# A decayed linear attention and two gated MLPs in one kernel: the last two attention chunks as 64x64 quarters of TensorE

## The chip, the cores and the metric

The kernel runs on one core of a Trainium2 chip. Its engines work side by side, each through its own list of instructions: TensorE (PE; PEld is its weight load), VectorE (DVE), ScalarE (ACT), GpSimd (POOL) and SyncE (SP), which issues the DMAs. The metric is the device time of one execution in microseconds; lower is better.

## The reference

`x` is the output of a block-wise linear attention with a decay for each head, and two MLPs follow on it. B = 2 batches, H = 8 heads, S = 768 tokens, D = 64.

```python
for b in range(nb):                      # blocks of 64 tokens
    intra = np.einsum('bhic,bhjc->bhij', qb, kb) * Dmask[None]     # lam ** (i - j), 0 above the diagonal
    intra = np.einsum('bhij,bhjd->bhid', intra, vb)
    inter = np.einsum('bhid,bhde->bhie', qb * lam_pow[None], kv_state)
    out[:, :, sl] = intra + inter
    kv_state = lam_block * kv_state + np.einsum('bhsd,bhse->bhde', kb * rev_pow, vb)
...
a = x @ w_a                              # 1536x512 by 512x1536
b = x @ w_b
x = (a * b @ w_out)
...
h = np.maximum(np.maximum(x @ w1, x @ w2), x @ w3)                 # 1536x512 by 512x768
return (h @ w_out)
```

## The kernel before

**Attention.** The kernel works on chunks of C = 128 tokens, NC = 6 of them for each batch. `n` numbers chunk and batch (n = 2m + b), and `pair(m)` is chunk m of both batches. For each n: `scores` multiplies keys with queries (PE), `masked` multiplies the result with the decay table (DVE, tiles `am`), `queries` and `keys` scale operands (POOL, in the tiles `aq` and `av`), `earlier` multiplies the running state `held` with the scaled queries (the state product, into the PSUM banks `o`), `within` adds the values, `taken` copies `o` into `x` (ACT), `update` multiplies scaled keys with values (into the bank `k`), and `carry` folds that into `held` (DVE; the tile is called `stt`). Heads are kept in halves of 64 partitions. From the fourth chunk on (`c >= SHORT`) `scores` leaves out the corner that the mask makes zero, and small bf16 matmuls on `warm` write zeros there, since `masked` still reads the whole square.

**First MLP.** Weights arrive as int64 words of 64-bit floats (`wr`), are converted to fp32 (`w` or `wd`, by three ACT passes and one DVE pass that joins them), combined by subtractions for a Strassen scheme, and split into a high and a low part (`hi` by an ACT copy, `lo` by a DVE or POOL subtraction); `x` is split in the same way (`x1A` are the parts of the second half of the tokens, `x0S` the parts of sums `x0s` of the first half). Every product is three matmuls: high by high, high by low, low by high. `plain_group` makes the first groups without Strassen; each `yield` of it is one layer block of 12 matmuls of 128x384 (L721, PSUM bank `p`), whose first half of columns ACT copies away (`z`) and whose second half DVE multiplies with it (`g`). The groups after that run seven products each (L701, banks `zu`, `bu`, `xu`).

**What sets the order.** The program is written out engine by engine. For PE, the loop over m at the end of the function writes the order down: scores, `next(layer1)` once or twice (one layer block each), `earlier`, `within`, `taken`, `update`, `carry`. `operands(1)` after the last chunk queues the splitting of x1. The work of ACT, DVE and POOL that isn't written out (weights, sums, splits) is placed between by `Pace`, a running estimate of each engine's time: a task's next step is issued when the estimate says that its engine is free. So other costs in the calls of `pace.pe` and `pace.run` move such steps to other places in the engines' lists, and sometimes from POOL to DVE (`EITHER`).

**PSUM.** There are eight banks, given out in turn. `results(m, apart)` takes two banks of `o` for a pair, or four when `apart`, which before holds for the last chunk alone.

Of the kernel before, what the change touches and what calls it, by code (L numbers as in the profile page):

```python
# [15 lines left out]
ALU = mybir.AluOpType  # L16
# [20 lines left out]
NPLAIN = 2  # L37
BYDVE = ()
SHORT = 3
NS = 26  # L40


# [126 lines left out]
def decay_attention_gated_mlps(ctx: ExitStack, tc: tile.TileContext, qkv: bass.AP, lam: bass.AP, wup: bass.AP, wdown: bass.AP, out: bass.AP):  # L169
# [9 lines left out]
    def slot(name, dt=F32):  # L179
        return sp.tile([128, 1536], dt, tag="s", name=name)  # L180
# [4 lines left out]
    def bank(name):  # L185
        return pp.tile([128, 512], F32, tag="ps", name=name)
# [7 lines left out]
    def copy(o, a):  # L194
        nc.scalar.activation(out=o, in_=a, func=AF.Copy)  # L195
# [267 lines left out]
    def pair(m):  # L463
        return 2 * m, 2 * m + 1
# [22 lines left out]
    def scores(n):  # L487

        q, k = aq[n][:, 0:512], aq[n][:, 512:1024]
        sc[n] = [bank(f"s{n}_{i}") for i in range(2)]  # L490
        if order[n][1] < SHORT:
            for a in range(NP):
                o = slice(128 * a, 128 * a + 128)
                for i in range(2):
                    nc.tensor.matmul(sc[n][i][:, o], k[rows(i), o], q[rows(i), o], start=True, stop=True)
            pace.pe(0.9, at["aq", n])
            return
        for a, late in ((0, 0), (0, 1), (1, 1), (1, 0), (2, 0), (2, 1), (3, 0), (3, 1)):
            for i in range(2):
                js = slice(128 * a + 64 * late, 128 * a + 64 * late + 64)  # L500
                o = slice(128 * a + 64 * late, 128 * a + 128)
                nc.tensor.matmul(sc[n][i][rows(late ^ a // 2), o], k[rows(i), js], q[rows(i), o], start=True, stop=True)  # L502
            if late and a % 2:
                p = a // 2
                for i in range(2):
                    o = sc[n][i][rows(1 - p), 256 * p:256 * p + 256].rearrange("p (a i) -> p a i", a=2)[:, :, 0:64]
                    nc.tensor.matmul(o, warm[rows(i), 0:64], warm[rows(i), 0:128], start=True, stop=True)
        pace.pe(0.8, at["aq", n])

    def masked(n):  # L510

        am[n] = slot(f"am{n}")
        for i in range(2):
# [20 lines left out]
        at["qs", n] = beside(512, at["aq", n])  # L534

    def keys(n):
        k, o = (av[n][:, x:x + 512].rearrange("p (h d) -> p h d", h=H) for x in (0, 1024))
        nc.gpsimd.tensor_tensor(out=o, in0=k, in1=decay[:, :, C - 1:C].to_broadcast([128, H, D]), op=ALU.mult)
        at["kd", n] = beside(512, at["av", n])
# [12 lines left out]

    def earlier(n):

        q = aq[n][:, 1024:1536]
        for w in range(2):
            for i in range(2):
                for x in range(2):
                    a = 2 * w + x
                    nc.tensor.matmul(  # L560
                        place(n, 4 * i + a), held[rows(i), n % 2, a], q[rows(i), 128 * a:128 * a + 128],
                        start=ob[n][1] == 0 and w == 0, stop=False, skip_group_check=True)
        pace.pe(0.5, max(at["qs", n], at["st"]))

    def within(n):

        v = av[n][:, 512:1024]
        for w in range(2):
# [9 lines left out]
    def update(n):  # L578

        if n % 2 == 0:  # L580
# [10 lines left out]
    def carry(m):  # L591

        src = kv[m].rearrange("p (b a e) -> p b a e", b=B, a=NP)
# [16 lines left out]
    def taken(n, *to):  # L610
        b, c = order[n]
        j = c // 3
        for x, name, dt in zip((xa, xh, xl), ("x", "xh", "xl"), (F32, F32R, F32R)):
            if (j, b) not in x and (j == 0 or x is xa):
                x[j, b] = slot(f"{name}{j}{b}", dt).rearrange("p (a i) -> p a i", a=KD)
        for x in to:
            for i in range(2):
                copy(tokens_of(x, n, i), result(n, i))
                at["x", n, i] = pace.run("ACT", 256, pace.t["PE"])
# [110 lines left out]
                    pace.run("DVE", J)  # L730
                yield

    def add(o, ps, z):
        nc.vector.tensor_tensor(out=o, in0=ps, in1=z, op=ALU.add)  # L734
        return pace.run("DVE", J)

    def tokens(j, b):
        return slice((2 * j + b) * J, (2 * j + b) * J + J)
# [210 lines left out]
    with tc.manual_schedule():  # L949
# [196 lines left out]
        for m in range(3, NC):  # L1146
# [27 lines left out]
            if m == 3:  # L1174
                pace.open(("x0", "sums"))
            if not last:
                for n in pair(m):
# [180 lines left out]
```

## Time and profile before

| | us |
|---|---|
| median of 3 runs | 502.0 (501.64 to 502.49) |
| span of the profiled execution, first to last instruction | 500.4 |
| PE busy | 493.1 |
| DVE busy | 345.8 |
| ACT busy | 293.9 |
| POOL busy | 58.1 |

For the profiled execution the trace gives the span; the device time of a run takes in what lies around it, and the median is 1.6 us above this span. Busy time is the union of an engine's instructions. A matmul's row starts when it begins to stream and lasts until its result is through, so successive matmuls overlap, and their rate is read from the distance of their starts.

### The profile page before, as it was taken

The page shows a single profiled execution, that of the slowest core. Times are in us where ns is not written, and L with a number is a line of the kernel's source. Part 1 is how long each engine was busy: PE and PEld are TensorE (multiplying, and loading weights), DVE is VectorE, ACT ScalarE, POOL GpSimd, SP SyncE. Part 2 cuts the span into 40 slices and gives each one's busy share as a digit, 9 for nine tenths or more (in the row PEclk, how much of TensorE's full clock was granted, in tenths as well). Part 3 has the DMA queues.
Part 4 walks back from the last instruction along what each step waited for, and adds up shares of the span by engine and source line. Part 5 has one row for each costly group of instructions (what it writes and reads, how often), then busy time and mean ns, then how long its engine had stood idle before and what let it go on. Part 6 is the DMA issues. An engine that isn't in the chain of part 4 may idle for free.

```text
span 500.4 us, 8186 instructions
## 1 busy us (share of the span) xinstructions
PE 493.1 (99%) x3348; PEld 465.0 (93%) x3348; DVE 345.8 (69%) x541; ACT 293.9 (59%) x458; POOL 58.1 (12%) x55
## 2 busy tenths in 40 slices
PE   8899999999999999999999999999999999999997
PEld 6799999999999999998888888999999999998897
DVE  6779869576576567567365079568877985787962
ACT  2677565564656553769572477545756456576461
POOL 3685301011111101110000000000000000000000
PEclk9999999999999999999999999999999999999999
DMA  8997002222221112314322021002202212110023
GB/s 285 407 410 270 3 0 85 84 85 84 86 84 59 35 56 64 126 54 151 134 84 86 0 84 56 29 1 84 67 20 84 86 63 64 63 65 0 22 106 126
DMA packets 10693, 46.93 MB, mean 94 GB/s; under 512 B 1312, under 2 KB 1568, under 8 KB 8096
## 3 DMA queue, kind: packets, MB, share of 16 engines
q1 hardware_dynamic: 10656, 46.41, 25.7%
q8 instruction: 26, 0.43, 0.4%
q14 instruction: 11, 0.09, 0.1%
HBM read 43.26 MB, written 3.15 MB: 93 GB/s over the span
## 4 chain that ended last, share of the span: by engine, by line
PE 95%; DMA 2%; DVE 1%; SPq 1%; issue 0%; ACT 0%
PE yp L820 20%; PE zu L701 18%; PE zv L701 15%; PE bu L701 9%; PE bv L701 7%; PE p L721 5%; PE out L874 5%; PE xu L701 4%; PE xv L701 4%; PE zo L923 3%; DMA av<-qkv_dram 2%; PE o L573 1%; PE bo L923 1%; PE s L502 1%; SPq L480 1%; PE xo L923 1%
## 5 line engine op out<-in xcount | busy, mean ns | idle before, releaser
L192 DVE TENSOR_TENSOR lo<-w,hi 128x1024 fp32r<-128x1024 f32 (+2 forms) x39 | 42.7, 1094 | 11.5 <-ACT hi L195 11.3
L195 ACT ACTIVATE hi<-w 128x1024 fp32r<-128x1024 f32 (+2 forms) x40 | 37.4, 935 | 14.2 <-DVE w L192 6.3
L820 PE MATMUL yp<-gh,dh 128*128 128x512 f32 x108 | 42.0, 389 | 0.0
L820 PE MATMUL yp<-gl,dh 128*128 128x512 f32 x108 | 42.0, 389 | 0.0
L820 PE MATMUL yp<-gh,dl 128*128 128x512 f32 x108 | 42.0, 389 | 0.0
L752 POOL TENSOR_TENSOR g<-z1u,z6u 128x384 f32<-128x384 f32 x21 | 22.6, 1076 | 148.2 <-DVE z6u L734 148.2
L192 DVE TENSOR_TENSOR gl<-g,gh 128x512 fp32r<-128x512 f32 x36 | 25.2, 720 | 20.7 <-ACT gh L195 20.7
L238 DVE SCALAR_TENSOR_TENSOR w<-ws,w 128x1024 int32<-128x1024 int32 (+1 forms) x21 | 30.7, 1464 | 9.6 <-ACT w L227 7.8
L227 ACT ACTIVATE w<-wr 128x1024 f16<-128x1024 f32 (+2 forms) x26 | 33.1, 1274 | 0.3
L192 DVE TENSOR_TENSOR w<-w 128x256 f32<-128x256 f32 (+1 forms) x57 | 30.1, 527 | 1.3
L222 ACT ACTIVATE w<-wr 128x1024 int32<-128x1024 uint16 (+2 forms) x26 | 27.5, 1056 | 2.4 <-DVE lo L192 2.0
L734 DVE TENSOR_TENSOR z6u<-bu,z6u 128x384 f32<-128x384 f32 x21 | 11.7, 556 | 21.0 <-PE bu L701 21.0
L195 ACT ACTIVATE gh<-g 128x512 fp32r<-128x512 f32 x36 | 21.4, 621 | 7.4 <-PE yp L820 7.4
L195 ACT ACTIVATE z6u<-zu 128x384 f32<-128x384 f32 x21 | 10.2, 484 | 24.9 <-PE zu L701 24.9
L820 PEld LDWEIGHTS yp<-gh,dh 128*128 128x128 f32 x108 | 20.3, 188 | 4.2
L820 PEld LDWEIGHTS yp<-gl,dh 128*128 128x128 f32 x108 | 20.3, 188 | 4.2
L230 ACT ACTIVATE ws<-wr 128x1024 f32<-128x1024 f32 (+1 forms) x22 | 24.1, 1094 | 0.2 <-DMA wr<-wup_dram 0.2
L820 PEld LDWEIGHTS yp<-gh,dl 128*128 128x128 f32 x108 | 20.3, 188 | 4.1
L195 ACT ACTIVATE z7u<-zu 128x384 f32<-128x384 f32 x21 | 10.3, 491 | 22.5 <-PE zu L701 22.5
L701 PE MATMUL bu<-x1S,hi 128*128 128x384 f32 x88 | 22.3, 334 | 0.0
L701 PE MATMUL zu<-x1S,hi 128*128 128x384 f32 x88 | 22.3, 334 | 0.0
L701 PE MATMUL zu<-x1A,hi 128*128 128x384 f32 x84 | 21.3, 334 | 0.0
(251 smaller groups left out, 1448.4 us busy)
## 6 DMA issues: line engine op xcount, KB each, us to landing
wr<-wup_dram SPq DMA_DIRECT2D x20, 1024.0 KB, 4.8
wr<-wdown_dram SPq DMA_DIRECT2D x12, 768.0 KB, 4.3
aq<-qkv_dram SPq DMA_DIRECT2D x12, 512.0 KB, 7.7
av<-qkv_dram SPq DMA_DIRECT2D x7, 512.0 KB, 11.0
out_dram<-ob SPq DMA_DIRECT2D x11, 256.0 KB, 2.0
av<-qkv_dram SPq DMA_DIRECT2D x7, 256.0 KB, 7.8
wr<-wup_dram SPq DMA_DIRECT2D x2, 512.0 KB, 9.7
out_dram<-ob SPq DMA_DIRECT2D x2, 128.0 KB, 1.9
```

Source lines behind the costliest of these rows:

```text
L192: (nc.vector if e == "DVE" else nc.gpsimd).tensor_tensor(out=o, in0=a, in1=b, op=op)
L195: nc.scalar.activation(out=o, in_=a, func=AF.Copy)
L222: nc.scalar.activation(out=w.bitcast(I32), in_=halves[:, :, 1], func=AF.Copy, scale=2.0 ** -13, bias=2.0 ** -14 - 0.5)
L227: nc.scalar.activation(out=o[:, :, 1], in_=high(double), func=AF.Copy, scale=2.0 ** -112)
L230: nc.scalar.activation(out=near, in_=high(double), func=AF.Copy, scale=2.0 ** -112)
L238: nc.vector.scalar_tensor_tensor(out=w, in0=near, scalar=3, in1=w, op0=ALU.logical_shift_left, op1=ALU.bitwise_or)
L701: nc.tensor.matmul(ps, w, x, start=p in FIRST and i == 0, stop=i == len(todo) - 1, skip_group_check=p not in FIRST)
L721: nc.tensor.matmul(ps, w[:, 128 * k:128 * k + 128], x[:, k], start=m == 0, stop=m == 11)
L752: nc.gpsimd.tensor_tensor(out=ga[g.n][:, tokens(g.j, 0)], in0=g.z[1], in1=g.z[6], op=ALU.mult)
L820: nc.tensor.matmul(ps[e], w[:, cols], g, start=k == 0 and m == 0, stop=k == K1 - 1 and m == 2)
L874: nc.tensor.matmul(ps, a[:, o:o + 128], w[:, s], start=k == 0 and n == 0, stop=k == K2 - 1 and n == 2)
L923: nc.tensor.matmul(ps, x[:, 128 * r:128 * r + 128], w, start=p in FIRST and n == 0, stop=n == 8, skip_group_check=p not in FIRST)
```

## The change

With `QUARTERS = 4`, the chunks c = 4 and 5 (n = 8 to 11) are computed on tiles of 64x64. On the host, keys and values of these chunks are laid out so that one half of the partitions holds both token halves of a head. Scores are written without the masked corner and without the zeros that filled it, 384 columns for four heads in place of 512; `near_table` copies the decay table in that form (four ACT copies after the fourth chunk's masks); `masked` multiplies 384 columns; `within` and `update` contract over 64 tokens at a time, in two halves of the partitions and two banks. Where the state product of a head and its values come from different partition halves, they land in different banks, and `taken` copies one (ACT) and adds the other (DVE). Both chunks take four banks for `o`. In the fifth chunk one of the two layer blocks moves from before the state product to between values and update.

```diff
@@ tables and masks
+    near = sttab[:, 640:1408].rearrange("p (h i) -> p h i", h=NP)
...
+    def near_table():
+
+        far = decay.rearrange("p (i r c) n -> p r i c n", i=2, r=2)
+        close = near.rearrange("p (i c) n -> p i c n", i=2)
+        for r in range(2):
+            s = slice(64 * r, 64 * r + 64)
+            for o, w in ((0, C), (C, 64)):
+                copy(close[s, :, :, o:o + w], far[s, r, :, :, 0:w])
+                pace.run("ACT", 4 * w)
...
@@ scores
+        if order[n][1] >= QUARTERS:
+            for c in range(2):
+                for late in range(2):
+                    for r in range(2):
+                        for p in range(2):
+                            a = 128 * (2 * r + c)
+                            nc.tensor.matmul(
+                                sc[n][p][rows(r), 192 * c + 128 * late:192 * c + 128 + 64 * late],
+                                k[rows(p), a + 64 * late:a + 64 * late + 64], q[rows(p), a + 64 * late:a + 128], start=True, stop=True)
+            pace.pe(0.65, at["aq", n])
+            return
@@ masked
+            for p in range(2):
+                nc.vector.tensor_tensor(out=am[n][:, 384 * p:384 * p + 384], in0=sc[n][p][:, 0:384], in1=near[:, 2 * p:2 * p + 2].rearrange("p h i -> p (h i)"), op=ALU.mult)
...
@@ earlier
+            for across in (1, 0):
+                for c in range(2):
+                    for p in range(2):
+                        r = p ^ across
+                        a, o = 2 * r + c, 256 if across else 128 * p
+                        nc.tensor.matmul(
+                            ob[n][0][p][rows(c), o:o + 128], held[rows(p), n % 2, a], aq[n][rows(p), 1024 + 128 * a:1152 + 128 * a],
+                            start=bool(across), stop=False, skip_group_check=True)
@@ within
+            for p in range(2):
+                for late in range(2):
+                    for c in range(2):
+                        for r in range(2):
+                            o, s = 256 * late + 128 * p + 64 * c, 384 * p + 192 * c + 128 * late
+                            nc.tensor.matmul(
+                                ob[n][0][r][rows(c), 128 * p + 64 * late:128 * p + 128], v[rows(r), o:o + 64], am[n][rows(r), s:s + 128 - 64 * late],
+                                start=False, stop=p == 1 and late == 1, skip_group_check=True)
+            pace.pe(0.7, max(at["av", n], at["am", n]))
+            return
@@ update
+                kv[n // 2] = [bank(f"k{n}_{i}") for i in range(2)]
...
+                            nc.tensor.matmul(
+                                kv[n // 2][r][rows(p), o:o + 64], k[rows(r), s:s + 64], v[rows(r), s:s + 64],
+                                start=n % 2 == 0 and c == 0 and late == 0, stop=n % 2 == 1 and c == 1 and late == 1, skip_group_check=True)
@@ taken
+        if c >= QUARTERS:
+            blocks = [xa[j, b][:, a, C * (c % 3):C * (c % 3) + C] for a in range(KD)]
+            banks = ob[n][0]
+            for r in range(2):
+                copy(blocks[2 - r], banks[1 - r][:, 256:384])
+                pace.run("ACT", 128, pace.t["PE"] - 0.7)
+            for r in range(2):
+                copy(blocks[3 * r], banks[r][:, 128 * r:128 * r + 128])
+                pace.run("ACT", 128, pace.t["PE"])
+                add(blocks[2 - r], banks[r][:, 128 - 128 * r:256 - 128 * r], blocks[2 - r], 128)
+            return
@@ the loop over the chunks
-            for _ in range(1 if last else 2):
+            if m == QUARTERS - 1:
+                near_table()
+            for _ in range(2 if m < QUARTERS else 1):
                 next(layer1)
-            results(m, last)
+            results(m, m >= QUARTERS)
...
             if not last:
+                if m >= QUARTERS:
+                    next(layer1)
                 for n in pair(m):
                     update(n)
                 carry(m)
```

The change moves instructions in the lists of DVE and ACT. The first place is DVE's list from the sixth chunk's masks (`am`) to the first low part of x1 (`x1A`), which the first layer block on x1 reads; `lo` is a weight's low part, `x0S` the low part of a sum of x0, `g` the product at a block's end. Before:

```order
L514 TENSOR_TENSOR am_868<-s_0_844,tables 128x512
L514 TENSOR_TENSOR am_868<-s_1_845,tables 128x512
L192 TENSOR_TENSOR wd_553<-wd_553 128x256
L192 TENSOR_TENSOR x0S_885<-x0s_431,x0S_885 128x768
L192 TENSOR_TENSOR wd_553<-wd_553 128x256
L192 TENSOR_TENSOR x1A_933<-x_610,x1A_933 128x768
```

And now:

```order
L538 TENSOR_TENSOR am_892<-s_1_875,stt 128x384
L193 TENSOR_TENSOR lo_910<-w_745,hi_909 128x1024
L193 TENSOR_TENSOR x0S_629<-x0s_431,x0S_629 128x768
L193 TENSOR_TENSOR lo_910<-w_745,hi_909 128x768
L822 TENSOR_TENSOR x_613<-o_0_914,x_613 128x128
L822 TENSOR_TENSOR x_613<-o_1_915,x_613 128x128
L822 TENSOR_TENSOR x_616<-o_0_916,x_616 128x128
L822 TENSOR_TENSOR x_616<-o_1_917,x_616 128x128
L193 TENSOR_TENSOR x0S_631<-x0s_431,x0S_631 128x768
L817 TENSOR_TENSOR g_705<-p_988,z_912 128x384
L193 TENSOR_TENSOR x1A_984<-x_613,x1A_984 128x768
```

The low parts of weight item 2 (`lo_910`; before, `lo_771` stood ahead of the masks on DVE and on POOL), two x0 sums and g now stand between the masks and x1A, beside the four new additions.

The second place is ACT's list in the same stretch, from weight item 2's high parts (`hi`) to x1's. Before:

```order
L195 ACTIVATE hi_770<-w_705 128x1024
L195 ACTIVATE x_610<-o_0_751 128x2x128
L195 ACTIVATE x_610<-o_1_752 128x2x128
L195 ACTIVATE x_613<-o_0_751 128x2x128
L195 ACTIVATE x_613<-o_1_752 128x2x128
L195 ACTIVATE hi_770<-w_705 128x768
L195 ACTIVATE z_886<-p_871 128x384
L195 ACTIVATE x0S_885<-x0s_431 128x768
L195 ACTIVATE x_610<-o_0_888 128x2x128
L195 ACTIVATE x_610<-o_1_889 128x2x128
```

And now:

```order
L196 ACTIVATE z_912<-p_895 128x384
L196 ACTIVATE hi_909<-w_745 128x1024
L196 ACTIVATE hi_909<-w_745 128x768
L196 ACTIVATE x_613<-o_1_915 128x128
L196 ACTIVATE x_613<-o_0_914 128x128 x2
L196 ACTIVATE x_613<-o_1_915 128x128
L196 ACTIVATE x_616<-o_1_917 128x128
L196 ACTIVATE x_616<-o_0_916 128x128 x2
L196 ACTIVATE x_616<-o_1_917 128x128
L196 ACTIVATE x1A_984<-x_613 128x768
```

The two high parts of item 2 went from ahead of z to behind it.

The third place is ACT's list some 30 us later, around the high parts of weight item 3, of which the Strassen groups' product 5 is the first to read the upper 768 columns; z6u and z7u are copies of products 6 and 7 of the group before. Before:

```order
L195 ACTIVATE z1u_1_1155<-zu_1_1148 128x384
L195 ACTIVATE hi_1167<-w_1067 128x1024
L195 ACTIVATE z6u_1_1184<-zu_1_1148 128x384
L195 ACTIVATE hi_1167<-w_1067 128x768
L230 ACTIVATE ws_1204<-wr_727 128x1024
L195 ACTIVATE z7u_1_1212<-zu_1_1148 128x384
```

And now:

```order
L196 ACTIVATE z1u_1_1210<-zu_1_1203 128x384
L196 ACTIVATE z6u_1_1237<-zu_1_1203 128x384
L196 ACTIVATE hi_1229<-w_1133 128x1024
L196 ACTIVATE z7u_1_1263<-zu_1_1203 128x384
L196 ACTIVATE hi_1229<-w_1133 128x768
L196 ACTIVATE z1u_0_1276<-zu_0_1269 128x384
```

Each of the two high parts moved behind one more z copy.

## Rows read from the trace of the kernel before

**Rows 1.** The page: span, and busy time of PE and PEld with its share

```profile
span 500.4 us, 8186 instructions
PE 493.1 (99%) x3348; PEld 465.0 (93%) x3348; DVE 345.8 (69%) x541; ACT 293.9 (59%) x458; POOL 58.1 (12%) x55
```

**Rows 2.** Waits of PE: us in total, times, longest

```profile
PE warm_ps L972 <- ACT stt L967: 2.4, 1, 2.4
```

**Rows 3.** Busy us by stretch: length, PE, PEld, DVE, ACT, POOL, PEclk, DMA share, GB/s

```profile
50.00:100.00 50.00, 50.00 (x399) 48.95 (x396) 38.90 (x59) 28.92 (x46) 7.29 (x5) 1.00 0.12 43
```

**Rows 4.** Timeline of PE, fourth chunk: start us, us, operation, count

```profile
36.31 1.10 PE L560 MATMUL o<-aq,stt 64*64 64x128 f32 x32
37.34 1.97 PE L573 MATMUL o<-am,av 128*64 128x128 f32 x32
39.14 1.10 PE L586 MATMUL k<-av 128*64 128x64 f32 x32
40.17 0.55 PE L502 MATMUL s<-aq 64*64 64x128 f32 x14
...
41.78 0.44 PE L721 MATMUL p<-xh,hi 128*128 128x384 f32 x1
```

**Rows 5.** Timeline of PE, sixth chunk

```profile
53.64 0.34 PE L721 MATMUL p<-xh,lo 128*128 128x384 f32 x1
...
54.94 1.97 PE L573 MATMUL o<-am,av 128*64 128x128 f32 x32
56.84 0.45 PE L721 MATMUL p<-xh,hi 128*128 128x384 f32 x1
57.12 0.34 PE L721 MATMUL p<-xl,hi 128*128 128x384 f32 x1
...
59.03 0.59 PE L721 MATMUL p<-x1A,hi 128*128 128x384 f32 x2
59.46 0.33 PE L721 MATMUL p<-x1A,lo 128*128 128x384 f32 x1
```

**Rows 6.** Timeline of ACT, fifth and sixth chunk

```profile
44.17 0.49 ACT L195 ACTIVATE z<-p 128x384 f32<-128x384 f32 x1 [0.26 <-PE p L721]
44.56 0.84 ACT L195 ACTIVATE x0S<-x0s 128x768 fp32r<-128x768 f32 x1
...
48.08 1.06 ACT L195 ACTIVATE hi<-w 128x1024 fp32r<-128x1024 f32 x1 [0.30 <-DVE w L192]
49.04 1.19 ACT L195 ACTIVATE x<-o 128x256 f32<-128x256 f32 x4
...
54.02 0.49 ACT L195 ACTIVATE z<-p 128x384 f32<-128x384 f32 x1 [3.05 <-PE p L721]
```

**Rows 7.** Timeline of DVE, end of the attention

```profile
49.57 1.22 DVE L192 TENSOR_TENSOR lo<-w,hi 128x1024 fp32r<-128x1024 f32 x1
50.71 0.95 DVE L192 TENSOR_TENSOR x0S<-x0s,x0S 128x768 fp32r<-128x768 f32 x1
51.57 1.12 DVE L599 SCALAR_TENSOR_TENSOR stt<-stt,tables,k 128x128 f32<-128x128 f32 x4
...
59.91 0.55 DVE L729 TENSOR_TENSOR g<-p,z 128x384 f32<-128x384 f32 x1
60.38 0.95 DVE L192 TENSOR_TENSOR x1A<-x,x1A 128x768 fp32r<-128x768 f32 x1
```

**Rows 8.** Timeline of POOL: the sixth chunk's queries, both batches

```profile
43.45 3.52 POOL L533 TENSOR_TENSOR aq<-aq,tables 128x512 f32<-128x512 f32 x2
```

**Rows 9.** Timeline of ACT, item 3's upper 768 columns

```profile
85.04 0.83 ACT L195 ACTIVATE hi<-w 128x768 fp32r<-128x768 f32 x1
...
87.61 0.49 ACT L195 ACTIVATE z7u<-zu 128x384 f32<-128x384 f32 x1 [0.71 <-PE zu L701]
```

**Rows 10.** Timeline of PE, the product 5 that reads them

```profile
88.45 0.51 PE L701 MATMUL bu<-x0S,hi 128*128 128x384 f32 x2
88.80 0.33 PE L701 MATMUL bu<-x0S,lo 128*128 128x384 f32 x1
```

More of the change, by code (lines that the diff above doesn't have):

```diff
@@ L39 @@
 SHORT = 3
+QUARTERS = 4
 NS = 26
@@ L512, in masked @@
         am[n] = slot(f"am{n}")
+        if order[n][1] >= QUARTERS:
+            for p in range(2):
+                nc.vector.tensor_tensor(out=am[n][:, 384 * p:384 * p + 384], in0=sc[n][p][:, 0:384], in1=near[:, 2 * p:2 * p + 2].rearrange("p h i -> p (h i)"), op=ALU.mult)
+                at["am", n] = pace.run("DVE", 384, pace.t["PE"])
+            sc.pop(n)
+            return
         for i in range(2):
@@ L536, in keys @@
     def keys(n):
+        if order[n][1] >= QUARTERS:
+            k, o = (av[n][:, x:x + 512].rearrange("p (l h d) -> p l h d", l=2, h=NP) for x in (0, 1024))
+            ends = near.rearrange("p h (x i) -> p x h i", x=3)[:, 1:3, :, 63:64]
+            nc.gpsimd.tensor_tensor(out=o, in0=k, in1=ends.to_broadcast([128, 2, NP, D]), op=ALU.mult)
+            at["kd", n] = beside(512, at["av", n])
+            return
         k, o = (av[n][:, x:x + 512].rearrange("p (h d) -> p h d", h=H) for x in (0, 1024))
@@ L553, in earlier @@
     def earlier(n):
+        if order[n][1] >= QUARTERS:
+            for across in (1, 0):
[6 more added lines that the diff above has]
+                            start=bool(across), stop=False, skip_group_check=True)
+            pace.pe(0.5, max(at["qs", n], at["st"]))
+            return
         q = aq[n][:, 1024:1536]
@@ L567, in within @@
         v = av[n][:, 512:1024]
+        if order[n][1] >= QUARTERS:
+            for p in range(2):
[7 more added lines that the diff above has]
+            pace.pe(0.7, max(at["av", n], at["am", n]))
+            return
         for w in range(2):
@@ L578, in update @@
     def update(n):
+        if order[n][1] >= QUARTERS:
+            if n % 2 == 0:
+                kv[n // 2] = [bank(f"k{n}_{i}") for i in range(2)]
+            v, k = av[n][:, 512:1024], av[n][:, 1024:1536]
+            for c in range(2):
+                for late in range(2):
+                    for p in range(2):
+                        for r in range(2):
+                            s, o = 256 * late + 128 * p + 64 * c, 128 * (n % 2) + 64 * c
+                            nc.tensor.matmul(
+                                kv[n // 2][r][rows(p), o:o + 64], k[rows(r), s:s + 64], v[rows(r), s:s + 64],
+                                start=n % 2 == 0 and c == 0 and late == 0, stop=n % 2 == 1 and c == 1 and late == 1, skip_group_check=True)
+            pace.pe(0.47, at["kd", n])
+            return
         if n % 2 == 0:
@@ L591, in carry @@
     def carry(m):
+        if m >= QUARTERS:
+            for a in range(NP):
+                src = kv[m][a // 2][:, 0:256].rearrange("p (b a e) -> p b a e", b=B, a=2)[:, :, a % 2]
+                nc.vector.scalar_tensor_tensor(out=held[:, :, a], in0=held[:, :, a], scalar=ahead[:, a, C - 1:C], in1=src, op0=ALU.mult, op1=ALU.add)
+                at["st"] = pace.run("DVE", 128, pace.t["PE"] if a == 0 else 0.0)
+            return
         src = kv[m].rearrange("p (b a e) -> p b a e", b=B, a=NP)
@@ L615, in taken @@
                 x[j, b] = slot(f"{name}{j}{b}", dt).rearrange("p (a i) -> p a i", a=KD)
+        if c >= QUARTERS:
[4 more added lines that the diff above has]
+                pace.run("ACT", 128, pace.t["PE"] - 0.7)
+            for r in range(2):
+                copy(blocks[3 * r], banks[r][:, 128 * r:128 * r + 128])
+                pace.run("ACT", 128, pace.t["PE"])
+                add(blocks[2 - r], banks[r][:, 128 - 128 * r:256 - 128 * r], blocks[2 - r], 128)
+            return
         for x in to:
@@ L731, in plain_group, with add @@
                 yield
-    def add(o, ps, z):
+    def add(o, ps, z, n=J):
         nc.vector.tensor_tensor(out=o, in0=ps, in1=z, op=ALU.add)
-        return pace.run("DVE", J)
+        return pace.run("DVE", n)
     def tokens(j, b):
@@ L1176, in decay_attention_gated_mlps @@
             if not last:
+                if m >= QUARTERS:
+                    next(layer1)
                 for n in pair(m):
@@ L1319, with by_token @@
     kt[:, :SHORT, :, :, 2:] = np.roll(kt[:, :SHORT, :, :, 2:], 64, axis=5)
-    parts = [x.reshape(B * NC, 128, 512) for x in (chunks_t(q), kt, turned(chunks_n(k)), turned(chunks_n(v)))]
+    def by_token(a):
+        quarters = a.reshape(B, 2, 2, 2, NC, 2, 64, D).transpose(0, 4, 2, 6, 5, 1, 3, 7).reshape(B, NC, C, H, D)
+        return np.where((np.arange(NC) < QUARTERS)[:, None, None, None], turned(chunks_n(a)), quarters)
+    parts = [x.reshape(B * NC, 128, 512) for x in (chunks_t(q), kt, by_token(k), by_token(v))]
     qkv = np.ascontiguousarray(np.stack([np.concatenate(parts[0:2], axis=2), np.concatenate(parts[2:4], axis=2)], axis=1))
```

## The prediction

> **What bounds the kernel now.** I read the page first: the span is 500.4 us and TensorE (PE) is busy for 493.1 of them [rows 1]. The waits of PE come next: the longest, 2.4 us, is at the very start, before any data [rows 2]. In the stretch from 50 to 100 us, which holds the end of the attention, PE is busy for all 50 us at a granted clock of 1.00, its upper level of 2.4 GHz [rows 3]. So PE is the bound where the change acts: a microsecond of matmuls removed there is a microsecond won, but only if nothing that PE reads comes late, and a microsecond for which PE is made to wait is lost for good, since no later idle time takes it up. The two questions are what the quarters save on PE, and whether ScalarE (ACT) and VectorE (DVE) still deliver in time in their new order.
>
> **What the quarters save on PE.** Each fp32 matmul leaves two records. Values (L573), before, run as rounds of two in the two column halves: 32 records from 37.34 to 39.14, so 16 rounds of 0.1125 us [rows 4]. The state product (L560) already runs as rounds of four quarters: 8 rounds in 1.03 us, 0.90 of which is 8 x 0.1125 and the rest the change of tile form [rows 4]. The update (L586) has 16 rounds of two with 64 columns in 1.03 us, 0.0645 each [rows 4]. After, the values of a pair are 8 rounds of four with 128 columns and 8 with 64: 0.90 + 0.52 = 1.42 in place of 1.80, 0.38 less. Scores of a pair have the same 16 rounds, 1.42 plus 0.13 for the change of form, in place of 1.61 with the eight filler matmuls of the masked corner [rows 4]; I take 0.1 less. The update keeps 16 rounds, now of four: no change if four fit into 0.0645. No row shows four with 64 columns. The bound from the other side is the scores' own rate, 64 fp32 records and 8 fillers by the code in 1.61 us, or 0.022 each [rows 4]: four would take 0.09, which makes the update 0.4 slower and each shorter round 0.025 slower, 0.2 per stage, in all 1.2 us, enough to eat the whole gain. The nearest row is that of L560, where four side by side cost no more than two, so I take no loss and keep 1.2 for the range.
>
> The layer block between values and update costs changes of form: a block behind values starts 1.90 us after them (54.94 to 56.84), where the update started after 1.80; the block's first step is 0.28 in place of 0.17 [rows 5]; leaving it I price at another 0.1. That is 0.3 more. Against it, state product, values, update and scores now share one form, at up to 0.13 for each change saved (two before values, one before scores). These cancel within 0.1. The sum for PE alone: 2 x 0.38 + 2 x 0.1 = **1.0 us less**.
>
> A rule of the Trainium skill speaks against the short rounds: TensorEngine Tiling (Array Packing), under Instruction Overhead, says that each matmul has about 60 cycles of overhead and that no tiling factor should be taken from a dimension that is already small. Read as 0.025 us that the four matmuls of a round pay in turn, it would make a round of 64 columns 0.10, and the sum for PE 0.7 us more instead of 1.0 less, by estimate. The scores' 0.022 for each record, with two tile forms running side by side, lies below that, so the trace does not bear this reading out.
>
> **What is added beside PE, and where it hides.** The table's four copies on ACT (two of 512, two of 256 wide) lie between the widths of 0.30 (four of 256 in 1.19) and 0.84 (768) [rows 6]: some 1.7 us. The weight conversion behind them, and with it DVE's low part for the next block, comes 1.7 us later, and I find it done about 0.5 us before PE asks for it, so nothing; without that margin it would cost up to 0.8. GpSimd scales the sixth chunk's queries behind a 512-wide weight subtraction now; two such operations took 3.52 us [rows 8]. By the walk they end about 1 us before PE's state product, at 1.3 each; with one at 2.3 the margin is gone. Eight masks of 384 in place of 512 columns are cheaper. The eight additions and sixteen narrow copies are priced below, where they matter.
>
> **Where a wait appears: the first use of x1.** Let S be the start of the last matmul of the block ahead of the sixth chunk's state product: 53.64 before [rows 5]. Before, the first block that reads x1A (59.03) comes at S + 5.39 [rows 5]. After, the values between are 0.4 shorter, so PE gets there at S + 4.95 and needs the low part at S + 5.12. In the changed order ACT takes that block's z copy first, then both high parts of weight item 2 (1024 and 768 wide; before, the first of them began at 48.08, well ahead of z [rows 6]), then the eight narrow copies. DVE has the matching low parts, an x0 sum, the additions, another x0 sum and g ahead of x1A's low part; before, none of the weight parts stood there. The walk: z starts at S + 0.38 (54.02) and frees ACT 0.39 later (44.17 to 44.56); the 1024-wide high part takes 1.06 and ends at S + 1.83 [rows 6]. DVE: low part 1.14 (49.57 to 50.71), to S + 2.97; x0S 0.86 (50.71 to 51.57), to 3.83; 768-wide low part 0.86, to 4.69; the additions at 0.28 each (nearest: four 128-wide operations out of PSUM in 1.12), the second done at 5.25 [rows 7]. ACT's high part of x1A, 0.84 [rows 6], ends at 6.1, so PE first waits about 1.2. DVE meanwhile: two more additions to 5.8, x0S to 6.67, g 0.47 to 7.14 (59.91 to 60.38), the low part 0.95, to 8.09 [rows 7]. Each hand-over costs some 0.04 (the block's last matmul ends at 53.98, z starts at 54.02); five of them make 8.3. Before, PE lost 0.08 there (59.46 less 59.03 is 0.43, two steps are 0.35) [rows 5]. So the second x1A matmul comes 8.3 - 5.1 - 0.1 = **3.1 us late**. Only PE itself is queued behind it, which is the bound.
>
> **A second one, in the first Strassen groups.** Item 3's upper 768 columns were made at 85.04, ahead of the z7 copy at 87.61 [rows 9]; now they stand behind it. z7 is set by PE: 87.61, plus 0.39, plus 0.83 gives 88.83, where PE wants them at 88.45; the low part is ready 0.95 later, at 89.78, where PE then would be at 88.80 + 0.38 [rows 10, 7]. That is 0.4 + 0.6 = **1.0 us**, on any clock time, since both ends move with PE.
>
> **Sum:** 500.4 - 1.0 + 3.1 + 1.0 = 503.5 for the profiled execution. The median of the runs lies 1.6 above the span; with that, **505.1 us**.
>
> **Rivals.**
> 1. *The queues hide it; faster.* PE's gain stays and x1A is in time if DVE reaches its low part by S + 4.2, four microseconds sooner than in my walk. For this the item 2 parts would have to be done before z, as they were at 48.08; the order speaks against it. It gives 501.0. Chance 5%. The Trainium skill states the queues of ScalarE, VectorE and GpSimd as strictly first in, first out (PSUM — Partial Sum Buffer, Engine vs sequencer instructions); by that this rival is out.
> 2. *Only the evacuation counts.* Tile outputs leave by eight copies and four additions in place of four 256-wide copies (1.19) [rows 6]. Alone, and not behind the weight parts, they would end x1A's first addition near S + 3.4, its high part at 4.3, its low part at 5.3: 0.2 of waiting, or 501.2; with the second wait 502.2. Chance 7%. This is what the Trainium skill's PSUM Bottleneck would give (TensorEngine Tiling): tiling speeds up TensorE, not the evacuation.
> 3. *Only the first wait, the second absorbed* because item 3's upper part is ready in some other way: 504.1. Chance 15%.
> 4. *More waits*: rounds of four limited to 0.09 (up to 1.2), queries late (up to 1), or TensorE's clock falling during the waits. The trace holds 1.00 through a wait of 2.4 [rows 2, 3]; this one is longer in sum but broken by one matmul. About 506.5. Chance 15%.
> 5. The likeliest, both waits as walked: 504.3 to 506.0, chance 58%.
>
> **Numbers.** The runs of before spread over 0.85 us, so 0.2%, or 1.0 us, is about what can be told from no change. Rivals 1 and a part of 2 are within or below it: faster 6%, same 5%, slower 89%. The range leaves out rivals 1 and 2 and the far end of 4: 503.2 to 506.8.
>
> **What would show it.** Right: the values of the last two pairs take about 1.4 us between first records; PE stands still before the first and the second x1A matmul, released by ACT and by DVE, about 3 us together, and again before item 3's product 5, about 1 us; DVE runs the two low parts between the sixth chunk's masks and its additions. Wrong: x1A's low part starts within a microsecond of the additions, PE has no gap over 0.5 us near 58, or the 64-column rounds take 0.09 or more.

## The result and the profile after

The changed kernel takes 507.56 us (median of 4 runs, 506.05 to 508.07), the kernel before 501.89 beside it: a ratio of 1.0107, interval 1.0095 to 1.0119. It is 5.7 us slower where 3.1 were forecast, outside the range. The profiled execution has a span of 506.2 us, 5.8 more than [rows 1].

The page after (span; busy time of the engines; PE's clock in 40 slices, in tenths; one DMA queue with packets, MB and share):

```profile
span 506.2 us, 8374 instructions
PE 494.9 (98%) x3428; PEld 465.7 (92%) x3428; DVE 346.7 (68%) x550; ACT 296.0 (58%) x470; POOL 54.3 (11%) x54
...
PEclk9999989999999999999999999999999999999999
...
q8 instruction: 27, 0.44, 0.4%
```

PE is busy for 1.8 us more than before, although its matmuls should take 1.0 less: one slice, the sixth, has a lower clock. The waits of PE after (us in total, times, longest) answer to [rows 2]:

```profile
PE warm_ps L1060 <- ACT stt L1055: 2.4, 1, 2.4
PE p L809 <- DVE x1A L193: 1.3, 1, 1.3
...
PE p L809 <- ACT x1A L196: 1.1, 1, 1.1
PE o L620 <- issue: 0.6, 1, 0.6
PE bu L789 <- DVE lo L193: 0.4, 1, 0.4
...
PE p L809 <- DVE lo L193: 0.4, 1, 0.4
PE bu L789 <- ACT hi L196: 0.3, 1, 0.3
```

Four of these lines are the two waits that were forecast, x1A and product 5 (bu). Two were not: one for a low part (the first block's, near 42 us), and one at the values (L620) that no engine releases. The two lines left out are waits for input DMAs ahead of the fourth chunk, 1.6 us together; the kernel before had as much there in its profiled execution. PE's timeline shows the places (start us, us, operation, count, idle time ahead), to be held against [rows 4, 5, 10]:

```profile
42.35 0.44 PE L809 MATMUL p<-xh,lo 128*128 128x384 f32 x1 [0.36 <-DVE lo L193]
...
45.24 0.27 PE L620 MATMUL o<-am,av 64*64 64x128 f32 x1
...
45.35 0.92 PE L620 MATMUL o<-am,av 64*64 64x128 f32 x28
46.84 1.02 PE L620 MATMUL o<-am,av 64*64 64x64 f32 x35 [0.57 <-issue]
47.80 0.44 PE L809 MATMUL p<-xh,hi 128*128 128x384 f32 x1
...
50.10 1.16 PE L646 MATMUL k<-av 64*64 64x64 f32 x64
51.08 1.52 PE L509 MATMUL s<-aq 64*64 64x128 f32 x64
52.53 0.45 PE L809 MATMUL p<-xh,hi 128*128 128x384 f32 x1
...
55.74 1.52 PE L620 MATMUL o<-am,av 64*64 64x128 f32 x64
57.19 0.45 PE L809 MATMUL p<-xh,hi 128*128 128x384 f32 x1
...
60.69 0.44 PE L809 MATMUL p<-x1A,hi 128*128 128x384 f32 x1 [1.14 <-ACT x1A L196]
62.41 0.44 PE L809 MATMUL p<-x1A,hi 128*128 128x384 f32 x1 [1.28 <-DVE x1A L193]
...
63.91 0.52 PE L809 MATMUL p<-x1A,lo 128*128 128x384 f32 x1
64.23 0.84 PE L809 MATMUL p<-x1A,hi 128*128 128x384 f32 x2
64.87 0.52 PE L809 MATMUL p<-x1A,lo 128*128 128x384 f32 x1
...
93.48 0.62 PE L789 MATMUL bu<-x0S,hi 128*128 128x384 f32 x2 [0.27 <-ACT hi L196]
94.48 0.44 PE L789 MATMUL bu<-x0S,lo 128*128 128x384 f32 x1 [0.37 <-DVE lo L193]
```

Read starts, not durations; a wait "by starts" is the distance of two starts less 0.174 us, the step of one such matmul. The sixth pair's values take 57.19 less 55.74, 1.45 us, where they took 1.90 [rows 5]; its scores 1.45, the update 0.98. The fifth pair's values take 2.56 (45.24 to 47.80), with a hole before 46.84. Behind the x1A waits three matmuls take 0.96 us (63.91 to 64.87), 0.32 each in place of 0.174 [rows 5]. The stretches say why (length, PE, PEld, DVE, ACT, POOL, PEclk, DMA share, GB/s):

```profile
59.00:63.50 4.50, 2.08 (x11) 1.51 (x10) 4.50 (x10) 3.05 (x4) 0.00 (x0) 1.00 0.00 0
63.50:67.00 3.50, 3.50 (x13) 3.50 (x12) 3.19 (x4) 1.55 (x3) 0.00 (x0) 0.51 0.00 0
67.00:85.00 18.00, 18.00 (x105) 18.00 (x105) 13.67 (x20) 10.28 (x17) 1.43 (x1) 1.00 0.17 59
```

PE stands still for more than half of 4.5 us. Then the granted clock is 0.51 over the 3.5 us of the second row: by the trace's record of the clock, the lower level of 1.2 GHz from 63.50 us on, for 3.4 us.

### The profile page after: what moved, and what is told of

It reads as the page before. It is cut to its first block, busy times and chain, and to the rows that moved or that the text cites. A ratio compares the mean times of both kernels' runs of the same rounds, so it can differ in the third digit from the quotient of the medians.

```text
span 506.2 us, 8374 instructions
## 1 busy us (share of the span) xinstructions
PE 494.9 (98%) x3428; PEld 465.7 (92%) x3428; DVE 346.7 (68%) x550; ACT 296.0 (58%) x470; POOL 54.3 (11%) x54
## 4 chain that ended last, share of the span: by engine, by line
PE 92%; DVE 2%; DMA 2%; SPq 1%; issue 1%; ACT 1%; DVEq 0%
PE yp L908 19%; PE zu L789 17%; PE zv L789 15%; PE bu L789 9%; PE bv L789 7%; PE p L809 5%; PE out L962 5%; PE xu L789 4%; PE xv L789 4%; PE zo L1011 3%; DMA av<-qkv_dram 2%; PE bo L1011 1%; DVE lo L193 1%; PE xo L1011 1%; SPq L492 1%
## 5 line engine op out<-in xcount | busy, mean ns | idle before, releaser
L193 DVE TENSOR_TENSOR lo<-w,hi 128x1024 fp32r<-128x1024 f32 (+2 forms) x40 | 43.8, 1095 | 12.1 <-ACT hi L196 11.8
L840 POOL TENSOR_TENSOR g<-z1u,z6u 128x384 f32<-128x384 f32 x21 | 24.3, 1158 | 154.1 <-DVE z6u L822 154.1
L239 DVE SCALAR_TENSOR_TENSOR w<-ws,w 128x1024 int32<-128x1024 int32 (+1 forms) x21 | 29.5, 1403 | 9.1 <-ACT w L228 7.5
L193 DVE TENSOR_TENSOR w<-w 128x256 f32<-128x256 f32 (+1 forms) x55 | 28.4, 517 | 1.2
```

The costliest lines, as they stand in the source:

```text
L193: (nc.vector if e == "DVE" else nc.gpsimd).tensor_tensor(out=o, in0=a, in1=b, op=op)
L239: nc.vector.scalar_tensor_tensor(out=w, in0=near, scalar=3, in1=w, op0=ALU.logical_shift_left, op1=ALU.bitwise_or)
L840: nc.gpsimd.tensor_tensor(out=ga[g.n][:, tokens(g.j, 0)], in0=g.z[1], in1=g.z[6], op=ALU.mult)
```

## The experiments

Theory A: PE waits because ACT and DVE deliver in a new order, and the clock falls behind the waits. Theory B: the quarters, or their evacuation, are slow in themselves. Theory C: the moved block is what costs. Each ratio is to the kernel before, timed on the same chip.

**The same kernel again (e1_again).**

> The changed kernel once more, to see which losses of its trace repeat. Every theory expects 507.5 us again. Theory A (PE waits because ACT and DVE deliver x1 and item 3 in a new order, and TensorE's clock falls behind the waits): the two waits before the first x1A matmuls (1.3 and 1.55 us), the 1.0 us at item 3's product 5 and the 3.4 us at a granted clock of 0.5 behind the x1A block all stand at the same places. If the fall of the clock or the 0.7 us gap in the fifth chunk's values near 46 us are chance events of one execution, they are gone and the span is 1.7 or 0.7 us shorter.

Measured: 507.37 us, ratio 1.0105 (1.0087 to 1.0123), five runs from 505.58 to 508.03. Its profiled execution has a span of 503.7 at a clock of 1.000. The x1A waits (1.30 and 1.55 by starts) and product 5 (0.97) stand at the same places, and so does the wait for the low part (0.56); the hole in the fifth pair's values has shrunk, and these take 1.93. The clock splits the executions: of the nine of both batches, five show a mean of 0.996 or 0.997 and spans of 505.4 to 506.2, the others 1.000 and 503.7, 504.2, 504.3 and once 505.6. The fall happens in about half of them. By the medians of these spans (505.9 and 504.25) it costs 1.65 us; half the rate for 3.4 us is 1.7. Single executions also differ in their start, so below I compare them from the fourth chunk's state product on, which lies ahead of what the change touches: 464.1 us before, 468.0 in e1, 470.2 in the profiled execution after.

**The moved block alone (e2_block_only).**

```
-            for _ in range(1 if last else 2):
+            for _ in range(2 if m < 4 else 1):
...
             if not last:
+                if m == 4:
+                    next(layer1)
```

> The kernel before with one part of the change: one layer block of the fifth chunk stands between its values and its update instead of ahead of the state product; no quarters. Theory A: the move itself costs nothing but changes of form, 0 to 0.3 us, so 501.9 to 502.2. Theory C (the moved block is what costs): 503 or more, with a wait at the update or at x1A.

Measured: 502.61 us, 1.0018 (1.0009 to 1.0027), 0.9 more, between the two windows. PE now waits at the sixth chunk's state product, for the state that DVE carries over, since one block only lies between:

```profile
PE o L560 <- DVE stt L599: 0.5, 1, 0.5
```

Theory C holds for 0.9 us here; in the changed kernel that wait does not appear.

**The block held back (e3_held).** The block between the fifth chunk's values and update goes behind the sixth chunk's values.

```
             if not last:
-                if m >= QUARTERS:
-                    next(layer1)
```

> The changed kernel, quarters and all, but the layer block between the fifth chunk's values and update is held back: it comes behind the sixth chunk's values, in front of the first block that reads x1A, and gives ACT and DVE 2.1 us more. Theory A: the x1A waits of 2.8 us and the fall of the clock (1.7 us) go; the wait at product 5 (0.4 to 1.0) and some new wait at the sixth chunk's scores (up to 1.1, their banks come free later) stay: 502.0 to 503.5, at a clock of 1.00. Theory B (the quarters or their eight copies and four additions are slow in themselves): it stays above 505.

Measured: 504.46 us, 1.0055 (1.0041 to 1.0069), clock 1.00 in all five. The x1A waits are gone. Three others have grown:

```profile
PE p L809 <- DVE lo L193: 1.5, 1, 1.5
PE bu L789 <- DVE lo L193: 0.7, 1, 0.7
...
PE s L509 <- issue: 0.6, 1, 0.6
```

The time lies 1 us above A's window and below B's bound, so it decides neither; the x1A waits and the fall of the clock went as A expects.

**PE kept busy (e4_fill).** Extra matmuls fill the x1A waits.

```
+                            if j == 1 and m == n == b == half == 0:
+                                for _ in range(7):
+                                    nc.tensor.matmul(ps, w[:, 0:128], xo[0].get("A11")[0][:, 0], start=True, stop=True)
+                                for _ in range(9):
+                                    nc.tensor.matmul(ps, w[:, 0:128], x[:, 0], start=True, stop=True)
```

> The changed kernel with 16 extra 128x384 matmuls that PE runs while it would wait: seven on old operands ahead of the first x1A matmul (7 x 0.174 = 1.22 us, the wait there is 1.3), and the first x1A matmul nine times more ahead of the second (1.57 us, the wait is 1.55). Their results are overwritten. The x1A operands come no sooner. If PE's standing still is what makes the clock fall: the granted clock stays at 1.00 behind it and the time falls by about 1.7 us, to 505.8. If the clock falls for another reason: it falls again, and the time stays at 507.5.

Measured: 506.23 us, 1.009 (1.0076 to 1.0104), 505.77 to 506.7. The clock stays at 0.999 or 1.000 in all four runs, and in the 21 runs of the four kernels below that keep the fill. That PE's standing still makes the clock fall is the reading that holds; the gain in the median is 1.1, since about half of the executions did not fall anyway.

**Only the first wait filled (e8_fill_first).** The same without the nine.

> The fill for the first of the two x1A waits alone: seven extra matmuls ahead of the first x1A matmul, none ahead of the second, which still waits 1.55 us. If one such wait is enough for the clock to fall in some executions: several of the six show a mean clock of 0.997 and take 1.7 us longer, the median between 506.2 and 507.5. If it takes both waits in a row: clock 1.00 in all of them, 506.2.

Measured: 506.16 us, 1.0097 (1.0084 to 1.011). One run of five fell (0.996, 507.93 us), so a fall does not seem to need both waits. Whether it is rarer behind one, five runs against nine can't tell.

**Item 3 first (e5_item3_first).** On top of the fill:

```
+            if p == 7 and (self.n, self.j) == (2, 1) and self.done is gated:
+                t = wtask[3]
+                while t.next is not None and t.next[0] != "gate":
+                    t.step(pace)
```

> The kernel with the fill (506.2 us) and, besides, item 3's upper columns (high part on ACT, low part on DVE) put ahead of the z7u copy that stands before product 5, as they were before the change. Nothing else moves. Theory A: the wait of 0.4 + 0.55 us at product 5 goes and with it 1.0 us: 505.2. Rival: TensorE finds the lost time again later, and 506.2 stays.

Measured: 505.45 us, 1.0073 (1.0061 to 1.0085). The wait at product 5 goes but for 0.19, and 0.8 us with it; from the fourth chunk on the profiled execution takes 467.2 us, against 468.1 with the fill alone. Nothing later takes it up.

**x0 sums later (e6_x0_late).** On top of the fill:

```
+            if m == 4:
+                pace.open(("x0", "sums"))
             results(m, m >= QUARTERS)
...
-            if m == 3:
-                pace.open(("x0", "sums"))
```

> The kernel with the fill (506.2 us) and, besides, the x0 sums opened one stage later, behind the fifth chunk's layer block, so that DVE makes item 1's low part ahead of them. Theory A (the table's copies make item 1 late on ACT, the planner then puts two x0 sums ahead of its low part, and DVE's second one is stretched from 0.95 to 1.92 us while POOL subtracts): the 0.56 us that PE waits for that low part near 42 us go, 505.7. Rival: the sums are late in their turn and hold up x0S or the values: 506.2 or more.

Measured: 505.08 us, 1.0073 (1.0058 to 1.0088), 1.15 less than the fill by the medians and 0.85 by the ratios; one of its six runs took 507.58 at a clock of 1.00, for which I have no cause (two of the 75 runs of the kernel before, 503.65 and 503.54 us, stand as far out at such a clock). The wait of 0.56 near 42 us is gone. From the fourth chunk on the profiled executions differ by 0.85 us (467.3 against 468.1), of which that wait is 0.6 and the fifth pair's values 0.1. What held DVE up is shown by the changed kernel's DVE and then its POOL:

```profile
38.26 0.95 DVE L193 TENSOR_TENSOR x0s<-x 128x768 f32<-128x768 f32 x1
39.24 1.92 DVE L193 TENSOR_TENSOR x0s<-x0s,x 128x768 f32<-128x768 f32 x1
41.08 1.21 DVE L193 TENSOR_TENSOR lo<-wd,hi 128x1024 fp32r<-128x1024 f32 x1
```

```profile
38.48 1.87 POOL L193 TENSOR_TENSOR wd<-wd 128x512 f32<-128x512 f32 x1 [1.22 <-DVE wd L239]
```

The second x0 sum ends 0.8 us behind POOL's subtraction (41.16 against 40.35), which is about what it takes alone: I read it as held until POOL was done. In this run, where the two no longer meet, the same sum takes 0.96 and the same POOL instruction 1.29.

**All three moved (e7_all_moved).** The held block, with item 3's step at p == 2 and the x0 sums later, without the fill.

> The kernel of the held block (504.46 us), with item 3's upper columns first and the x0 sums opened later. Theory A: of its waits, 1.5 us for item 1's low part and 0.9 at product 5 go; the one at the sixth chunk's scores (0.6, up to 1.4) stays: 502.0 to 502.8, so no better than before the change, since the quarters save only 0.8. Theory B (the quarters slow in themselves): above 503.5.

Measured: 502.30 us, 1.0009 (1.0000 to 1.0018): level with before. The waits that A names are gone, and theory B is out: quarters, copies and additions are all in it. What is left in the stages that the change touches is a hole:

```profile
PE s L509 <- issue: 1.3, 1, 1.3
```

**The block unmoved (e9_unmoved).**

```
-            for _ in range(2 if m < QUARTERS else 1):
+            for _ in range(1 if last else 2):
...
-                if m >= QUARTERS:
-                    next(layer1)
```

> The changed kernel with its quarters, but the layer block stays where it was, ahead of the fifth chunk's state product. Theory A (what the two engines are late with depends on the whole order): by a walk through the order of ACT and DVE the x1A waits become 0.8 and 1.7 us, the wait at product 5 is gone; 504.5 to 506.3, by whether TensorE's clock falls. Theory C (the moved block alone costs it): 502 or less.

Measured: 504.84 us, 1.0066 (1.0052 to 1.0081); one run of six fell (0.997). Product 5 does not wait, x1A waits once, for 1.5 us by starts, and the low part of 43.31 us for 1.6. The time is in A's window, but by luck: the walk had two waits at x1A, 0.8 and 1.7, and none for this low part. Theory C, 502 or less, is out: without the moved block the quarters still cost 3 us.

**Other planner costs, the same PE program (e10_planner_costs).**

```
-            pace.pe(0.65, at["aq", n])
+            pace.pe(0.8, at["aq", n])
...
-            pace.pe(0.7, max(at["av", n], at["am", n]))
+            pace.pe(0.9, max(at["av", n], at["am", n]))
...
-            pace.pe(0.47, at["kd", n])
+            pace.pe(0.5, at["kd", n])
```

> The changed kernel with the three TensorE costs that its planner assumes for scores, values and update set back to those of before (0.8, 0.9, 0.5 in place of 0.65, 0.7, 0.47). PE's instructions and their order stay the same to the last one; only the order on ACT, DVE and POOL differs. Theory A: by the walk the x1A waits become 2.0 and 0.8 us, the wait at product 5 is gone: 505.0 to 506.5. Theory B (the quarters are slow in themselves): 507.4 as it was.

Measured: 506.55 us, 1.0086 (1.0072 to 1.0099), three of five runs at 0.997. The time is at the edge of A's window, and its interval overlaps with that of the changed kernel; the waits decide. Not one instruction of PE differs, and the waits are others: 1.7 us for the first low part, which the walk did not have, 1.4 and 0.8 at x1A, where it had 2.0 and 0.8, none at product 5.

**PE's own program (e11_code_shift_32 and e12_code_shift_112).** The holes that nothing releases are left. A 16 KB transfer of the DMA queue q8 (its kind is "instruction") lands ahead of each; the queue's 0.44 MB are 64 B for each of the 6,856 records of PE and PEld, so I take it for PE's program: 16 KB are 256 records. In the kernel with the fill, small matmuls at the start move the code behind them against these transfers (here 32; the other has `keep_warm(1)` and 112).

```
-        keep_warm(5)
+        keep_warm(4)
+        for i in range(32):
+            nc.tensor.matmul(ps[:, 0:16], warm[:, 0:128], warm[:, 0:16], start=True, stop=True)
```

> The kernel with the fill (506.2 us), in which the fifth pair's values take 1.93 us from first record to the next block's, while the sixth pair's take 1.45. In the traces so far that loss grows the later a 16 KB instruction transfer starts ahead of these values (0.74 us ahead: 1.0 us lost; 1.3 to 1.6: 0.4 to 0.5; 2.0 or more: 0.1 or none). Here the last of the five warm-up matmuls is replaced by 32 of 16 columns, at the start of the program, where PE waits for data; PE's program from there on stands 62 instructions (4 KB) later, so the transfer should start about 3 us earlier, near 40.7 us in place of 43.9. If PE waits for its own instructions: the values take 1.45 us and the time falls by 0.4 to 0.5 us, to 505.8. If it is something else about these values: 1.9 us as before, 506.2.

> The same with 112 small matmuls in place of four of the five warm-up ones: 216 instructions, so that a boundary of 256 falls 40 instructions later than in the kernel with the fill, and the transfer starts some 0.8 us later, about 0.5 us ahead of the fifth pair's values. If PE waits for its own instructions: the values take 2.3 us or more, and the time rises by 0.4 to 0.7 us (and by what the small matmuls cost at the start, up to 2 us). If it is something else: 1.9 us as before.

Measured: 505.70 us with 32 (1.0079, 1.0067 to 1.0092), the fifth pair's values 1.64 in place of 1.93, not the 1.45 expected; 507.28 us with 112 (1.011, 1.0093 to 1.0126), the values 2.63, and a second hole at the sixth pair's scores (0.71 from start to start). Both intervals overlap with that of the fill, so the times alone show little. From the fourth chunk on the profiled executions take 467.7 and 469.6 us, against 468.1 with the fill; e12 loses another 1.3 us ahead of that, at its start, where the warm-up was changed. PE with 112:

```profile
46.53 1.26 PE L620 MATMUL o<-am,av 64*64 64x128 f32 x48
48.56 0.56 PE L620 MATMUL o<-am,av 64*64 64x128 f32 x15 [0.76 <-issue]
```

Data and semaphores are the same; the hole goes where the code boundary goes.

**The last hole (e13_all_moved_code_shift and e14_blocks_spread).** The first is the kernel with all three moved, with `keep_warm(1)` and 67 small matmuls. The second has one layer block ahead of the fourth, one ahead of the fifth chunk's state product, one between the fifth's values and update, one ahead of the sixth's scores, two behind its values, and the x0 sums later.

> The kernel with the held block, item 3 first and the x0 sums late (502.30 us), in which PE stands still for 1.3 us after 28 of the 64 records of the sixth pair's scores. Here 67 matmuls of 16 columns stand at the start in place of four of the five warm-up ones, so that PE's program stands 126 instructions later and a boundary of the instruction transfers no longer falls in the middle of these scores. If PE waits there for its own instructions: the gap shrinks to under 0.3 us and the time to 501.0 to 501.6 (less than 1.3 gained, since the small matmuls cost up to 0.5 at the start), which is below the 501.8 of before. If it waits for the PSUM banks that the fifth pair's additions free: the gap stays at the same place, 502.3 to 502.8.

> The quarters with one layer block wherever dense small matmuls meet: one ahead of the fourth and one ahead of the fifth chunk's state product, one between the fifth's values and update, one ahead of the sixth's scores, two behind the sixth's values; x0 sums late. If PE's instruction supply is what the dense stages lack: no gap without a releaser in any stage, and only small waits for masks, x1A and items (1.4 us together by the walk): 501.5 to 502.5. If it is the PSUM banks: the gap at the sixth pair's scores is gone as well, but the one in the fifth pair's values (0.4 to 1.0) stays.

Measured: 503.43 us (1.0023, 1.0012 to 1.0034) and 502.37 us (1.0008, 0.9997 to 1.0018). In the first the hole at the scores is gone (they take 1.49), as expected of a wait for instructions; but two others have opened, in the update and in the state product, and the time missed the 501.0 to 501.6 expected. Whether it is worse than with all three moved is unclear: the medians say 1.1 us, the intervals overlap, and from the fourth chunk on the profiled execution is shorter (464.6 against 465.0). Its waits:

```profile
PE k L646 <- issue: 1.0, 1, 1.0
PE o L596 <- issue: 0.6, 1, 0.6
```

In the second the time is as expected, but a hole of 0.5 from start to start is left in the fifth pair's values, which was the sign named for the PSUM banks. The places of the holes decide against the banks. From the traces' transfers and PE's next start, in us:

```
kernel   transfer starts, lands   PE goes on   behind the landing
after        44.50   45.55          46.84        1.29
e3           47.98   48.94          50.37        1.43
e7           46.52   47.53          49.03        1.50
e12          46.32   47.31          48.56        1.25
e12          51.55   52.52          53.80        1.28
e13          45.32   46.24          47.54        1.30
e13          50.92   51.88          53.10        1.22
e14          41.56   42.72          43.95        1.23
```

Count the records that each trace has ahead of the matmul with which PE goes on (a load and a matmul each, and PE's semaphore and drain entries): in all eight cases they are 192 or 193 more than a multiple of 256, be it in values, scores, update or state product. So the holes keep to one place in PE's program, counted in transfers of 16 KB, and not to one operation or bank.

## Why the prediction was wrong

The direction and the two waits were right, the size was not: 3.1 us forecast, 5.7 measured. Step by step:

- **PE's gain of 1.0.** Right where the code is there: the sixth pair's values 0.45 less, the scores 0.1 and 0.15, both state products about 0.1 each, the update 0.05, changes of form for the moved block 0.35 back; with fifth values of 1.34 and 1.43 (e9, e7) that is 1.0. Four matmuls side by side in a round of 64 columns cost no more than two ("I take no loss"). By the Trainium skill's rule of a fixed overhead for each matmul (TensorEngine Tiling (Array Packing), Instruction Overhead), read as paid in turn, the update would by estimate have taken 1.6; its 0.98 for 64 records does not agree. What no step of the sum had is that PE must also be handed these instructions: 0.5 us of the gain (1.1 in the profiled execution) is lost in the fifth pair's values.
- **"So nothing" for the table on ACT.** This step failed. The margin of 0.5 us was not there: item 1's low part, moved behind two x0 sums of which the second overlapped with POOL, made PE wait 0.56. The prediction shows no working for its margin; it prices like operations of DVE at 0.86 to 0.95, and this sum took 1.92. That stretch of 1.0 is nearly the whole way from a margin of 0.5 to a wait of 0.56. The price without the margin ("up to 0.8") was right. The Trainium skill says of GpSimd's SBUF interfaces that they are shared with VectorE, with contention for two SBUF inputs (GPSIMD Engine Reference, Specifications); the rows above agree, and it would have been worth a term.
- **x1A, 3.1 us.** Right in mechanism and near in size: 1.30 and 1.55, less 0.08 before, 2.8 us, the two low parts between masks and additions as walked.
- **Product 5, 1.0 us.** 0.97 by starts, 0.8 in the time when undone alone (e5).
- **The clock.** This is the largest failure. Rival 4 had it at 15% in all, on "The trace holds 1.00 through a wait of 2.4", and the sum had nothing for it. That reading was wrong. The wait stands at the very start, and this trace's record of the clock begins only at 6.33 us; the 1.00 that the page and the stretches give ahead of it has no record behind it. PE's timeline of the kernel before, below, shows the rate there: the 512-column matmuls behind the wait (L972) start 0.43 us apart, where those of the second MLP take 0.23, and the rounds of the first scores (L495) start 0.21 apart up to 6.3 us and 0.11 after: half the rate, as at the lower level, in this very trace. The waits at x1A come in the middle of work, and behind them the clock fell in five of nine executions, at some 1.7 us each. Over all kernels here in which PE waits at x1A, 10 of 25 runs fell; of the 76 runs of the other changed kernels none did, and of 75 of the kernel before one (0.996, 503.75 us), which I can't explain.

```profile
2.35 2.31 PE L972 MATMUL warm_ps<-stt 128*128 128x512 bf16 x5 [2.35 <-ACT stt L967]
4.66 2.83 PE L495 MATMUL s<-aq 64*128 64x128 f32 x32
...
11.34 2.06 PE L495 MATMUL s<-aq 64*128 64x128 f32 x32
```

- **The sum.** Without a fall: -0.5 for PE, 0.56, 2.8 and 0.97 make 3.8, against the 3.9 that e1 takes longer than the kernel before from the fourth chunk on (its span exceeds the profiled 500.4 by 3.3, and the 500.0 of the runs beside it by 3.7). With the fall, 5.5. So of the 2.6 us between forecast and measured, the clock is some 1.7, the low part 0.56 and the lost gain 0.5, less 0.3 at x1A. Rivals 1, 2 and 3 are out; that more waits come (rival 4) was the case, by the clock, but not by slow rounds of four or late queries. Its 506.5 comes nearest of all, for one of its three causes.

What stays open: why a given instruction transfer starts when it does, and why the same waits make the clock fall in one execution and not in the next. How far POOL's overlap alone made the low part late is argued from the rows; e6 took away the overlap and the order together.

## What to carry to other kernels

Matmuls saved on the engine that is the bound count only if every order that the saving shifts still delivers: walk each queue from the new order, with a price for operations that two engines run side by side. Price a wait on TensorE twice, once for itself and once for the clock behind it. Where many small matmuls follow one another, ask also whether the engine gets its instructions: the layer blocks between the dense stages seem to have given that time here, and a version without the waits for other engines came out level with the kernel before, not ahead. And before a row of a clock is taken as proof, see where its record begins.

## What the runs showed of the hardware

- In stretches of some 90 or more PE and PEld records in a microsecond PE stopped eight times with no releaser, at the same place in its program counted modulo 256 records, and went on 1.22 to 1.50 us behind the landing of a 16 KB transfer of the instruction queue. Moving the code by a few KB moved the holes: from the fourth chunk on, 0.4 us less and 1.4 more.
- After waits of 1.3 and 1.55 us with one matmul between, the mean clock was 0.996 or 0.997 in five of nine executions, in the profiled one by 3.4 us at the lower level; after one of 1.55 in one of five; with both filled in none of 25.
- Behind the wait of 2.4 us at the start, PE's scores ran at half the rate (0.21 us a round in place of 0.11) until the clock's record begins, at 6.33 us in the kernel before.
- A DVE operation with two inputs from SBUF, 0.96 us alone, took 1.92 beside one of POOL, and POOL's 1.87 in place of 1.29.
